# Order of the first batch: token-weight conversions placed behind the split of z, theta of block 1 ahead of attention of block 2

## The chip, the cores and the metric

One core of a Trainium2 chip runs one program. The metric is the device time of one execution in microseconds (us). TensorE (PE) multiplies matrices, VectorE (DVE) and ScalarE (ACT) do elementwise work, SyncE (SP) issues the transfers between memory and the on-chip buffers. Each engine works through its own list of instructions in the order in which they stand.

## The reference

All inputs are float32; batch B = 4, sequence S = 768, width 512 (8 heads of 64).

```python
# 1. attention by chunks of 32 queries; each sees 8 memory keys and a window of keys (16 left, 8 right)
a = softmax(q_c @ k_full.T / 8);  x = a @ v_full             # -> x[B, S, 512]
# 2. token mixing with a phase
theta = x @ w_theta
zr, zi = x * cos(theta), x * sin(theta)
y = w_tok_r @ zr + w_tok_i @ zi                              # over the 768 tokens
u = x + y;  x = u + relu(u @ w_ch)
# 3. gated block
h = gelu(x @ w_in);  u, v = halves of h
v = layernorm(v) * g_ln;  v = w_sg @ v + b_sg                # over the 768 tokens
out = x + (u * v) @ w_out
```

## The kernel before

**Precision.** A float32 operand of a matmul is split into a high part (rounded to the type float32r, by ScalarE) and a low part (operand minus high part, by VectorE). Each product is made of three: high by high, high by low, low by high.

**Tiles.** The 768 tokens of a batch are six blocks of 128. Blocks are counted from 0, over all batches. Per block the program runs, in functions of the same name:
- `att_s` (scores on PE into the PSUM tile `att2`, then maximum L245 and subtraction L247 on DVE, Exp L251 on ACT),
- `att_t` (transposes L258 of p on PE, copy L262 to `pt` on ACT),
- `att_v` (p times v on PE, again into `att2`; reciprocal of the row sum and L274 on DVE give x in `xt`),
- `att_x` (transposes L284 on PE, split into `xhi` by ACT L112 and `xlo` by DVE L113),
- `theta` (twelve matmuls L311; reduction to a turn, L322 and L325, on DVE into `t`; two Sin, L327 and L335, on ACT; z = x times them, L336, on DVE),
- `z_split` (high part L348 on ACT, two low parts L350 on DVE),
- `mix_group` (six matmuls L378 for each of four accumulators: 24 a block).

`att2`, `p`, `pt`, `t` and the PSUM tile of `theta` have one buffer each. The accumulators of mixing take all four buffers of `acc`, over all six blocks.

**Token weights.** `w_tok` comes as twelve pieces of 128x768 float64 values (six blocks for each half of the output tokens). `tok_conv` takes the next piece: it makes float32 high and low parts from the bits of the raw words, and asks for the load of the piece two further on (`raw` has three buffers, `cvh` two). Up to the second piece (`convert_pe`) the low part is made on PE, later (`convert`) on DVE: L150 and L203 on ACT, L153, L156, L160, L204, L208 and L209 on DVE. Mixing of block 0 with the first half needs the first piece, of block 1 the second, and so on.

**What sets the order.** `net_kernel` writes the work down step by step (the lines below), and a list scheduler takes that sequence as priorities. At each engine it takes the instruction of the highest priority whose operands it reckons to be there. So a line moved in the program changes the order of instructions on every engine, on SP's list of transfers too, also in places that the diff does not show. The first batch has a lead-in written out call by call, and then a loop over units `it` of mixing, with four groups `q` in each; `run` holds the pieces of attention, which are bound to a step and a group.

Of the kernel before, what the change touches and what calls it, by code (L numbers as in the profile page):

```python
# [32 lines left out]
def net_kernel(tc, qt, kw, vw, ident, w_theta, w_tok, w_ch, w_in, w_sg, w_out, g_ln, b_sg, out):  # L33
# [7 lines left out]
    AO, CO = -4, -2  # L41
# [8 lines left out]
    def r32(ap):  # L50
        return ap.bitcast(F32)
# [25 lines left out]
    def slot(n, tag, dtype=F32R):  # L77
        return w1.tile([128, n], dtype, tag=tag, name=tag, bufs=NBLK + 2)

    def two(t, i, n):  # L80
        return t[:, 2 * n * i:2 * n * i + 2 * n].rearrange("p (r t) -> p r t", r=2)
# [26 lines left out]
    def th_tile():  # L108
        return ps.tile([128, 512], F32, tag="th", name="th", bufs=1)

    def split(hi, lo, src, eng=None):
        nc.scalar.activation(out=hi, in_=src, func=AF.Copy)  # L112
        (eng or nc.vector).tensor_tensor(out=lo, in0=src, in1=r32(hi), op=ALU.subtract)  # L113
# [103 lines left out]
    def load_att(i):  # L217
        q = at.tile([128, NPAIR, 128], F32, tag="q", name="q", bufs=NQ)
        nc.sync.dma_start(out=q, in_=qt[i].rearrange("p (a t) -> p a t", a=NPAIR))
        q_t[i] = q  # L220
        nc.sync.dma_start(out=ka[i % NK], in_=kw[i])

    def load_v(i):
        nc.sync.dma_start(out=va[i % NKV], in_=vw[i])
# [71 lines left out]
    NFIRST = 2 * NBLK  # L296

    def has_theta(n):
        return 0 <= n < NBLK or NFIRST <= n < len(units)

    def theta(n):
        b, d0, nd, s, _ = units[n]
        xt, (_, xhi, xlo) = xt_of[b % 2][s], sets[b % 2]
        nz = 128 * nd
        cols = slice(128 * d0, 128 * d0 + nz)
        tok = slice(128 * s, 128 * s + 128)
        th = th_tile()[:, 0:nz]
        i = 0
        for k in range(KD):
            for a, w in ((xhi, th_hi), (xhi, th_lo), (xlo, th_hi)):  # L310
                nc.tensor.matmul(  # L311
                    out=th, lhsT=a[:, k, tok], rhs=w[:, k, cols],
                    start=(i == 0), stop=(i == 3 * KD - 1),
                )
                i += 1
        if n < NFIRST + 2:
            t = wk.tile([128, 512], F32, tag="t", name="t", bufs=1)[:, 0:nz]
        else:
            if len(t_slots) < 2:
                t_slots.append(slot(512, "slot_x", F32))  # L320
            t = t_slots[n % 2][:, 256 * (n // 2 % 2):256 * (n // 2 % 2) + 256]
        nc.vector.tensor_scalar(  # L322
            out=t, in0=th, scalar1=MAGIC, scalar2=MAGIC, op0=ALU.add, op1=ALU.subtract
        )
        nc.vector.tensor_tensor(out=t, in0=th, in1=t, op=ALU.subtract)  # L325
        z = wk.tile([128, 2, 512], F32, tag="z", name="z", bufs=ZB)[:, :, 0:nz]
        nc.scalar.activation(out=z[:, 1], in_=t, func=AF.Sin, scale=TWO_PI)  # L327
        if n < NBLK:
            nc.scalar.activation(out=z[:, 0], in_=t, func=AF.Abs)
        else:  # L330
            nc.vector.tensor_scalar(
                out=z[:, 0].bitcast(I32), in0=t.bitcast(I32), scalar1=0x7FFFFFFF, scalar2=None,
                op0=ALU.bitwise_and,
            )
        nc.scalar.activation(out=z[:, 0], in_=z[:, 0], func=AF.Sin, scale=-TWO_PI, bias=halfpi)  # L335
        nc.vector.tensor_tensor(  # L336
            out=z, in0=z, in1=xt[:, cols].unsqueeze(1).to_broadcast([128, 2, nz]), op=ALU.mult
        )
        sc_t[n] = z

    def z_split(n):
        z = sc_t.pop(n)
        if n < NBLK:
            a, b = slot(3 * 512, "slot"), slot(512, "slot_x")
            hi = two(a, 0, 512)
            lo = a[:, 1024:], b
            z_t[n] = z_t[n + NBLK] = (hi[:, 0], hi[:, 1]), lo
            nc.scalar.activation(out=hi, in_=z, func=AF.Copy)  # L348
            for i in range(2):
                (nc.gpsimd if n < -9 else nc.vector).tensor_tensor(  # L350
                    out=lo[i], in0=z[:, i], in1=r32(hi[:, i]), op=ALU.subtract
                )
            return
        if len(z_slots) < 2:
            z_slots.append(slot(3 * 512, "slot"))
        i = n % 3
        if i < 2:
            hi, lo = two(z_slots[i], 0, 256), two(z_slots[i], 1, 256)
        else:
            hi, lo = two(z_slots[0], 2, 256), two(z_slots[1], 2, 256)  # L360
        split(hi, lo, z)
        z_t[n] = (hi[:, 0], hi[:, 1]), (lo[:, 0], lo[:, 1])

    def mix_group(n, g):
        b, d0, nd, s, halves = units[n]
        d2, th = divmod(g, len(halves))
        th = halves[th]
        first, last = s == 0, s == NBLK - 1
        if first:
            acc_t[g] = acc_tile()  # L370
        zhi, zlo = z_t[n]
        whi, wlo = tok_w[s][th]
        acc = acc_t[g]
        zc = slice(128 * d2, 128 * d2 + 128)
        i = 0
        for ri in range(2):
            for z, w in ((zhi, whi), (zhi, wlo), (zlo, whi)):
                nc.tensor.matmul(  # L378
                    out=acc[:, 0:TC], lhsT=z[ri][:, zc], rhs=w[:, ri],
                    start=(first and i == 0), stop=(last and i == 5),  # L380
                )
                i += 1
        if last:
            _, xhi, xlo = sets[b % 2]
            dt = d0 + d2
            tt = slice(TC * th, TC * th + TC)
            u = wk.tile([128, TC], F32, tag="u", name="u", bufs=2)
            nc.vector.tensor_tensor(out=u, in0=acc[:, 0:TC], in1=r32(xhi[:, dt, tt]), op=ALU.add)
            (nc.gpsimd if b >= 4 else nc.vector).tensor_tensor(out=u, in0=u, in1=r32(xlo[:, dt, tt]), op=ALU.add)  # L389
            nc.sync.dma_start(out=u_dram[2 * b + th][:, dt, :], in_=u)  # L390
        if g == 3:
            z_t.pop(n)
# [237 lines left out]
    def run(it, slot):  # L630
        for fn, i in pieces.get((it, slot), []):
            if i < NA:
                fn(i)

    if True:
# [8 lines left out]
        def place(s):  # L644
            t = slot(3 * 512, "slot")
            tok_w[s][1] = two(t, 0, TC), two(t, 1, TC)
            xt_of[1][s] = slot(512, "slot_x", F32)
            w1s.pieces[NTH + NBLK + s] = tok_piece(s, 1)
# [31 lines left out]
        def tok_conv():  # L680
            nonlocal jw
            if jw >= NTH + NBLK:
                place(jw - NTH - NBLK)
            if jw < NTH + 2:
                w1s.convert_pe(jw, bank=acc_tile)
            else:
                w1s.convert(jw)
            w1s.load(jw + 2)
            jw += 1

        def att(part, i):
            part(i)
            if part is att_s:
                load_att(i + NK)
            if part is att_v:
                load_v(i + NKV)
# [10 lines left out]
        th_conv()  # L707
        theta(0)
        att(att_t, 1)
        tok_conv()  # L710
        att(att_v, 1)
        att(att_x, 1)
        z_split(0)
        att(att_s, 2)
        theta(1)
        tok_conv()
        att(att_t, 2)
        att(att_v, 2)
        z_split(1)
        att(att_s, 3)  # L720
        for it in range(NU):
            run(it, -2)
            run(it, -1)
            for q in range(4):
                if has_theta(it + 2) and q == (3 if it < NBLK else 0):
                    theta(it + 2)
                run(it, q)
                if it >= 0:
                    mix_group(it, q)
                if it < CO + NFIRST and q == 3:  # L730
                    tok_conv()
                if last_att + 2 <= it < last_att + 6 and q % 2:
                    j = 2 * (it - last_att - 2) + q // 2
                    p2["w"].convert(j)
                    p2["w"].load(j + NRAW)
                if has_theta(it + 2) and q == 3:
                    z_split(it + 2)
            run(it, 9)
            if it == NFIRST + CO - 1:
                close(st_cm)  # L740
                s1_cm, set1 = opened("set1")
                sets[1] = x_set(set1, 1, None)
            if it == last_att + 1:
                close(at_cm)
                close(s0_cm)
                open_p2()
                load_u(0)
                load_u(1)
                load_u(2)
            if it == last_att + 6:  # L750
                split_u(0)
# [142 lines left out]
```

## Time and profile before

| what | value |
|---|---|
| time, median of three runs (lowest to highest) | 758.88 us (755.14 to 758.88) |
| the profiled execution: its own time, its span | 762.43 us, 760.6 us |
| mean granted TensorE clock in the span | 0.993 of full speed |
| busy: PE / DVE / ACT | 730.4 us (96%) / 488.0 us (64%) / 306.9 us (40%) |
| chain that ended last: PE / DVE / DMA / ACT | 70% / 17% / 6% / 4% |

Busy shares are means over the whole span. The first 100 us or so, in which attention, theta, z and the conversion of token weights of the first batch all run, differ from the rest: there VectorE is nearly full as well. Times in the rows count from the start of the span. The end of a matmul is modelled, and instructions of one engine overlap a little, so that steps from start to start are what one of them costs.

### The profile page before, as it was taken

What the parts mean: (1) busy time and instruction counts of PE and PEld (TensorE: products, weight loads), DVE (VectorE), ACT (ScalarE), POOL (GpSimd) and SP (SyncE); (2) the same over time, 40 slices, a digit from 0 to 9 for tenths busy, and PEclk for the clock granted to TensorE, in tenths of its full rate; (3) what the DMA queues carried; (4) which work ended last, traced back from release to release, by engine and by line L of the source; (5) the groups of instructions that cost most, each with busy time, mean ns of one, the idle gap of its engine ahead of it and who ended that gap; (6) DMA issues with size and microseconds to landing.
All of it is one profiled execution on the core that took longest, in us unless ns stands there. A gap on an engine that the chain in (4) does not pass through costs nothing.

```text
span 760.6 us, 16131 instructions
## 1 busy us (share of the span) xinstructions
PE 730.4 (96%) x6968; PEld 680.7 (89%) x6968; DVE 488.0 (64%) x920; ACT 306.9 (40%) x470; POOL 0.3 (0%) x6
## 2 busy tenths in 40 slices
PE   5989999999999999999998899999999999999998
PEld 2667888889999999999998798999899989998997
DVE  4999898757566575798469777754355435543452
ACT  4867544554554554453125325611251134113310
POOL 0000000000000000000000000000000000000000
PEclk9998999999999999999999999999999999999999
DMA  8685465423323330341069755003100310030002
GB/s 345 226 288 163 151 224 182 142 72 129 123 85 127 112 113 30 102 177 43 11 226 328 276 185 158 1 0 115 53 1 1 114 53 1 1 125 0 1 1 84
DMA packets 33047, 86.90 MB, mean 114 GB/s; under 512 B 3792, under 2 KB 16208, under 8 KB 32976
## 3 DMA queue, kind: packets, MB, share of 16 engines
q1 hardware_dynamic: 30384, 77.22, 29.3%
q10 hardware_dynamic: 2592, 8.65, 3.6%
q8 instruction: 55, 0.90, 0.5%
q14 instruction: 16, 0.13, 0.1%
HBM read 66.98 MB, written 18.87 MB: 113 GB/s over the span
## 4 chain that ended last, share of the span: by engine, by line
PE 70%; DVE 17%; DMA 6%; ACT 4%; issue 2%; SPq 0%; DVEq 0%; ACTq 0%
PE acc L378 15%; PE acc L569 13%; PE acc L506 9%; PE acc L544 9%; PE acc L589 9%; PE th L311 7%; PE acc L432 3%; PE att L234 3%; DMA raw<-w_in 2%; DVE cvh L156 2%; DVE cvh L208 1%; DVE z L336 1%; PE att L258 1%; DVE cvm L204 1%; DVE u L389 1%
## 5 line engine op out<-in xcount | busy, mean ns | idle before, releaser
L378 PE MATMUL acc<-tok,slot 128*128 128x384 f32 x552 | 116.7, 342 | 2.5 <-ACT slot L348 2.5
L378 PE MATMUL acc<-slot 128*128 128x384 f32 x552 | 115.6, 340 | 0.0
L378 PEld LDWEIGHTS acc<-tok,slot 128*128 128x128 f32 x552 | 94.6, 188 | 4.6 <-ACT slot L348 2.8
L378 PEld LDWEIGHTS acc<-slot 128*128 128x128 f32 x552 | 95.5, 188 | 1.7
L569 PE MATMUL acc<-sg_hi,vlo 128*128 128x384 f32 x192 | 64.5, 336 | 0.0
L569 PE MATMUL acc<-sg_hi,vhi 128*128 128x384 f32 x192 | 64.4, 336 | 0.0
L569 PE MATMUL acc<-sg_lo,vhi 128*128 128x384 f32 x192 | 64.4, 336 | 0.0
L311 PE MATMUL th<-th_hi,xhi 128*128 128x256 f32 (+1 forms) x168 | 52.8, 314 | 1.6 <-ACT xhi L112 1.3
L112 ACT ACTIVATE ghi<-g 128x384 fp32r<-128x384 f32 x32 | 16.8, 525 | 88.0 <-DVE g L578 88.0
L311 PE MATMUL th<-th_hi,xlo 128*128 128x256 f32 (+1 forms) x168 | 51.4, 306 | 0.4 <-DVE xlo L113 0.4
L574 DVE SCALAR_TENSOR_TENSOR g<-acc,g_col,b_bc 128x384 f32<-128x384 f32 x32 | 19.8, 617 | 48.7 <-PE acc L569 48.7
L311 PE MATMUL th<-th_lo,xhi 128*128 128x256 f32 (+1 forms) x168 | 50.7, 302 | 0.0
L432 PE MATMUL acc<-ulo,ch_hi 128*128 128x384 f32 x128 | 43.7, 342 | 4.1 <-DVE ulo L113 4.1
L432 PE MATMUL acc<-uhi,ch_hi 128*128 128x384 f32 x128 | 43.7, 342 | 2.3 <-DVE x2e L438 2.3
L432 PE MATMUL acc<-uhi,ch_lo 128*128 128x384 f32 x128 | 43.4, 339 | 0.0
L544 PE MATMUL acc<-x3lo,in_hi 128*128 128x384 f32 x128 | 43.1, 336 | 0.0
L544 PE MATMUL acc<-x3hi,in_hi 128*128 128x384 f32 x128 | 43.1, 336 | 0.0
L544 PE MATMUL acc<-x3hi,in_lo 128*128 128x384 f32 x128 | 43.1, 336 | 0.0
L589 PE MATMUL acc<-glo,out_hi 128*128 128x384 f32 x128 | 43.0, 336 | 0.0
L589 PE MATMUL acc<-ghi,out_lo 128*128 128x384 f32 x128 | 43.0, 336 | 0.0
L589 PE MATMUL acc<-ghi,out_hi 128*128 128x384 f32 x128 | 42.9, 336 | 0.0
L595 DVE TENSOR_TENSOR o<-acc,x3f 128x384 f32<-128x384 f32 x32 | 17.8, 555 | 37.3 <-PE acc L589 37.3
(141 smaller groups left out, 1564.1 us busy)
## 6 DMA issues: line engine op xcount, KB each, us to landing
va<-vw SPq DMA_DIRECT2D x24, 520.0 KB, 4.0
ka<-kw SPq DMA_DIRECT2D x24, 512.0 KB, 4.8
raw<-w_tok SPq DMA_DIRECT2D x12, 768.0 KB, 5.1
q<-qt SPq DMA_DIRECT2D x24, 256.0 KB, 2.9
u_dram<-u SPq DMA_DIRECT2D x32, 192.0 KB, 2.1
uf<-u_dram SPq DMA_DIRECT2D x8, 768.0 KB, 7.9
x_dram<-x2e SPq DMA_DIRECT2D x32, 192.0 KB, 4.1
x3f<-x_dram SPq DMA_DIRECT2D x8, 768.0 KB, 4.7
```

Of the source, the lines that this page charges most:

```text
L112: nc.scalar.activation(out=hi, in_=src, func=AF.Copy)
L156: nc.vector.scalar_tensor_tensor(out=h, in0=high, scalar=-0x80000000, in1=h, op0=ALU.bitwise_and, op1=ALU.bitwise_or,)
L234: nc.tensor.matmul(out=out[32 * c:32 * c + 32, j, n * a:n * a + n], lhsT=lhs[h, a, 32 * c:32 * c + 32], rhs=rhs[h, 4 * a + c, :], start=Tr ...
L311: nc.tensor.matmul(out=th, lhsT=a[:, k, tok], rhs=w[:, k, cols], start=(i == 0), stop=(i == 3 * KD - 1),)
L378: nc.tensor.matmul(out=acc[:, 0:TC], lhsT=z[ri][:, zc], rhs=w[:, ri], start=(first and i == 0), stop=(last and i == 5),)
L432: nc.tensor.matmul(out=acc[:, 0:TC], lhsT=w[:, k, ee], rhs=x[:, k, :], start=(i == 0), stop=(i == 3 * KD - 1),)
L506: nc.tensor.matmul(out=acc, lhsT=x[:, k, tt], rhs=w[:, k, :], start=(i == 0), stop=(i == 3 * KD - 1),)
L544: nc.tensor.matmul(out=acc[:, 0:TC], lhsT=w[:, k, ff], rhs=x[:, k, :], start=(i == 0), stop=(i == 3 * KD - 1),)
L569: nc.tensor.matmul(out=acc[:, 0:TC], lhsT=v, rhs=w, start=(i == 0), stop=(i == 3 * NBLK - 1))
L574: nc.vector.scalar_tensor_tensor(out=g, in0=acc[:, 0:TC], scalar=p3["g"][:, f:f + 1], in1=p3["b"][:, tt], op0=ALU.mult, op1=ALU.add,)
L589: nc.tensor.matmul(out=acc[:, 0:TC], lhsT=w[:, k, ee], rhs=x[:, k, :], start=(i == 0), stop=(i == 3 * KD - 1),)
L595: nc.vector.tensor_tensor(out=o, in0=acc[:, 0:TC], in1=p3["xr"][c][:, e, :], op=ALU.add)
```

## The change

In the lead-in the first `tok_conv` goes behind `z_split(0)` and the second behind `att_t` of block 2; `theta(1)` goes ahead of `att_s` of block 2 and `z_split(1)` behind it. In the loop `tok_conv` of a step goes behind `z_split` of that step. No operation is added or removed.

```diff
         th_conv()
         theta(0)
         att(att_t, 1)
-        tok_conv()
         att(att_v, 1)
         att(att_x, 1)
         z_split(0)
+        tok_conv()
+        theta(1)
         att(att_s, 2)
-        theta(1)
+        z_split(1)
+        att(att_t, 2)
         tok_conv()
-        att(att_t, 2)
         att(att_v, 2)
-        z_split(1)
         att(att_s, 3)
...
-                if it < CO + NFIRST and q == 3:
-                    tok_conv()
...
                 if has_theta(it + 2) and q == 3:
                     z_split(it + 2)
+                if it < CO + NFIRST and q == 3:
+                    tok_conv()
```

What the scheduler makes of it is shown at three places. The number behind a tile's name tells buffers apart: `z_493` before and `z_452` after are z of block 1, `p_471` and `p_492` the scores of block 2, `cvh_747` and `cvh_752` the third piece of token weights, `cvh_902` and `cvh_907` the fourth, `att2_525` and `att2_530` the values of block 2.

ScalarE, from the high part of z of block 0 to the last Sin of block 1, before:

```order
L348 ACTIVATE slot_431<-z_354 128x1024
L150 ACTIVATE cvh_747<-raw_384 128x768
L251 ACT_TABLE_LOAD
L251 ACTIVATE p_471<-p_471 128x512
L190 ACTIVATE tok1_1_105<-acc_506 128x384
L190 ACTIVATE tok1_1_105<-acc_511 128x384
L327 ACT_TABLE_LOAD
L327 ACTIVATE z_493<-t_490 128x512
L329 ACTIVATE z_493<-t_490 128x512
L262 ACTIVATE pt_523<-att_518 128x512
L335 ACTIVATE z_493<-z_493,halfpi_98 128x512
```

The same stretch after:

```order
L348 ACTIVATE slot_411<-z_354 128x1024
L150 ACTIVATE cvh_752<-raw_434 128x768
L190 ACTIVATE tok1_1_105<-acc_518 128x384
L190 ACTIVATE tok1_1_105<-acc_523 128x384
L150 ACTIVATE cvh_907<-raw_528 128x768
L327 ACTIVATE z_452<-t_449 128x512
L329 ACTIVATE z_452<-t_449 128x512
L251 ACT_TABLE_LOAD
L251 ACTIVATE p_492<-p_492 128x512
L335 ACT_TABLE_LOAD
L335 ACTIVATE z_452<-z_452,halfpi_98 128x512
L262 ACTIVATE pt_508<-att_503 128x512
```

The Exp of block 2 with its table load stood ahead of both Sin of block 1; now it stands between them, with a table load on either side. The first step of the fourth piece (L150 on `raw_528`) has come ahead of the Sin, and the copy L262 of block 2 has gone behind the last Sin.

VectorE, from the subtraction of block 2's maximum to x of block 2, before:

```order
L247 TENSOR_TENSOR p_471<-att2_436,mx_469 128x2x4x64
L153 TENSOR_SCALAR cvh_747<-cvh_747 128x768
L322 TENSOR_SCALAR t_490<-th_477 128x512
L156 SCALAR_TENSOR_TENSOR cvh_747<-raw_384,cvh_747 128x768
L325 TENSOR_TENSOR t_490<-th_477,t_490 128x512
L160 TENSOR_SCALAR cvm_748<-cvh_747 128x768
L204 SCALAR_TENSOR_TENSOR cvm_748<-raw_384,cvm_748 128x768
L336 TENSOR_TENSOR z_493<-z_493,xt1_115 128x1024
L270 TENSOR_SCALAR rs_558<-att2_525 128x8
L208 TENSOR_TENSOR cvh_747<-cvh_747,tok0_2_106 128x768
L273 RECIPROCAL rs_558<-rs_558 128x8
L209 TENSOR_TENSOR tok1_2_107<-cvh_747,cvm_748 128x768
```

From the same instruction after:

```order
L247 TENSOR_TENSOR p_492<-att2_457,mx_490 128x2x4x64
L153 TENSOR_SCALAR cvh_752<-cvh_752 128x768
L153 TENSOR_SCALAR cvh_907<-cvh_907 128x768
L156 SCALAR_TENSOR_TENSOR cvh_752<-raw_434,cvh_752 128x768
L156 SCALAR_TENSOR_TENSOR cvh_907<-raw_528,cvh_907 128x768
L160 TENSOR_SCALAR cvm_753<-cvh_752 128x768
L160 TENSOR_SCALAR cvm_908<-cvh_907 128x768
L204 SCALAR_TENSOR_TENSOR cvm_753<-raw_434,cvm_753 128x768
L204 SCALAR_TENSOR_TENSOR cvm_908<-raw_528,cvm_908 128x768
L336 TENSOR_TENSOR z_452<-z_452,xt1_115 128x1024
L208 TENSOR_TENSOR cvh_752<-cvh_752,tok0_2_106 128x768
L270 TENSOR_SCALAR rs_563<-att2_530 128x8
```

Eight instructions of the third and fourth piece now stand between block 2's scores and z of block 1, where four of the third piece stood. L322 and L325 of block 1 have gone ahead of L247 (they stand just above these rows). Behind these rows L208 and L209 of the fourth piece follow around L274 of block 2, where before the fourth piece was only begun.

SyncE, the transfers from the second load of v for an odd block on, as a difference:

```order
 L221 DMA ka_123<-kw 128x1024
-L139 DMA raw<-w_tok 128x1536
 L224 DMA va_125<-vw 128x1040
+L139 DMA raw<-w_tok 128x1536 x2
 L219 DMA q<-qt 128x512
 L221 DMA ka_122<-kw 128x1024
```

The load of the third piece has gone behind a load of v, which waits until `att_v` of block 1 has read its buffer; the load of the fourth piece follows it at once, ahead of the keys and queries of block 4.

## Rows read from the trace of the kernel before

**Rows 1.** Windows: stretch, length, busy us of PE, PEld, DVE, ACT, POOL; clock; DMA.

```profile
100.00:120.00 20.00, 18.85 (x405) 16.95 (x405) 20.00 (x34) 7.84 (x11) 0.00 (x0) 1.00 0.70 229
...
220.00:300.00 80.00, 79.13 (x1153) 74.57 (x1152) 50.62 (x105) 41.84 (x63) 0.00 (x0) 1.00 0.32 103
```

**Rows 2.** Timeline of PE: start us, length us, instruction xcount, [idle before <- releaser].

```profile
36.71 1.04 PE L378 MATMUL acc<-tok,slot 128*128 128x384 f32 x5
...
43.54 1.69 PE L378 MATMUL acc<-tok,slot 128*128 128x384 f32 x8 [1.25 <-ACT slot L348]
...
57.73 0.63 PE L284 MATMUL att<-id_sb,xt 128*128 128x128 f32 x4 [2.25 <-DVE xt L274]
...
60.12 0.80 PE L311 MATMUL th<-th_hi,xhi 128*128 128x512 f32 x1 [0.65 <-ACT xhi L112]
...
66.20 0.86 PE L234 MATMUL att<-va,pt 64*32 64x65 f32 x64
67.00 1.14 PE L378 MATMUL acc<-tok,slot 128*128 128x384 f32 x5
...
91.18 2.00 PE L378 MATMUL acc<-tok,slot 128*128 128x384 f32 x10 [1.22 <-ACT slot L348]
```

**Rows 3.** Windows, PE alone: stretch, length, busy us, granted clock, DMA share, GB/s.

```profile
56.00:58.00 2.00, 0.27 (x3) 1.00 0.68 254
58.00:60.00 2.00, 1.47 (x68) 0.57 0.42 54
...
62.00:64.00 2.00, 2.00 (x8) 0.50 0.96 296
64.00:66.00 2.00, 2.00 (x8) 0.73 0.37 149
```

**Rows 4.** Timeline of PE, theta matmuls at either clock.

```profile
63.53 0.63 PE L311 MATMUL th<-th_lo,xhi 128*128 128x512 f32 x1
63.95 0.63 PE L311 MATMUL th<-th_hi,xlo 128*128 128x512 f32 x1
...
75.41 0.40 PE L311 MATMUL th<-th_hi,xlo 128*128 128x512 f32 x1
75.64 0.39 PE L311 MATMUL th<-th_hi,xhi 128*128 128x512 f32 x1
```

**Rows 5.** Timeline of ACT around the Sin of block 1.

```profile
37.44 1.28 ACT L327 ACT_TABLE_LOAD   x1
38.74 0.63 ACT L327 ACTIVATE z<-t 128x512 f32<-128x512 f32 x1
...
40.27 0.71 ACT L335 ACTIVATE z<-z,halfpi 128x512 f32<-128x512 f32 x1
...
42.44 1.05 ACT L348 ACTIVATE slot<-z 128x1024 fp32r<-128x1024 f32 x1
```

**Rows 6.** Timeline of DVE from z of block 1 to x of block 3.

```profile
41.02 1.23 DVE L336 TENSOR_TENSOR z<-z,xt 128x1024 f32<-128x1024 f32 x1 [1.11 <-ACT z L335]
...
43.39 0.96 DVE L209 TENSOR_TENSOR tok<-cvh,cvm 128x768 fp32r<-128x768 f32 x1
44.27 0.68 DVE L274 TENSOR_TENSOR xt<-att,rs 128x512 f32<-128x512 f32 x1
...
48.00 0.68 DVE L247 TENSOR_TENSOR p<-att,mx 128x512 f32<-128x512 f32 x1
...
49.67 0.55 DVE L153 TENSOR_SCALAR cvh<-cvh 128x768 int32<-128x768 int32 x1
50.14 0.95 DVE L204 SCALAR_TENSOR_TENSOR cvm<-raw,cvm 128x768 f32<-128x768 uint32 x1
...
56.90 0.68 DVE L274 TENSOR_TENSOR xt<-att,rs 128x512 f32<-128x512 f32 x1
```

**Rows 7.** The page's DMA issues, loads of token weights: xcount, KB each, us to landing.

```profile
raw<-w_tok SPq DMA_DIRECT2D x12, 768.0 KB, 5.1
```

**Rows 8.** Timeline of SP's queue: the load of v behind att_v of block 1.

```profile
28.83 0.33 SPq L224 DMA_DIRECT2D va<-vw  x1
```

## The prediction

> **What bounds the kernel now.** I read the windows first, to see which engine is full in which stretch. From 100 to 120 us VectorE is busy for all of 20 us and PE for 18.85; from 220 to 300 us PE is busy for 79.13 of 80 us and VectorE for 50.62 [rows 1]. So the two engines bound the first batch together, and behind it PE alone does. The change reorders the first batch only, and whatever makes PE late there arrives at the end undiminished, unless PE gets it back before some 125 us.
>
> Then I read PE's timeline for its gaps, since these are what a new order can win or add. Between 36 and 92 us the large ones are 1.25 us ahead of mixing block 1 (it waits for the high part of z), 2.25 us ahead of the transposes of block 3 (for x on VectorE), 0.65 us ahead of theta of block 3, and 1.22 us ahead of mixing block 5 [rows 2]. They add up to 5.37 us.
>
> Then I read the clock. In the stretch that holds the 2.25 us gap PE is busy for 0.27 of 2 us, still at a granted 1.00, which is 2.4 GHz. Behind it the clock goes to 0.50, 1.2 GHz: means of 0.57, 0.50 and 0.73 in windows of 2 us [rows 3]. Theta of block 3 runs in that time: from start to start its matmuls take 0.42 us there and 0.23 us at the full clock [rows 4]. Ten of them at 0.19 us more are 1.9 us that the gap costs beyond itself.
>
> **The change part by part.** All operations stay, so nothing is saved on any engine; only waits can change. I follow the new lists by hand from 36 us, with durations from start to start: L153 0.47 us, L204 0.87 (0.95 less the overlap of 0.08), L209 0.88, operations on 512 columns such as L274 0.60 (0.68 less 0.08) [rows 6]. L160 is taken like L153, L156 like L204 and L208 like L209, whose shapes they have.
>
> *Z of block 1.* VectorE now takes L322 and L325 of block 1 ahead of the scores of block 2, but theta itself waits for the same x as before, and mixing block 0, which started at 36.71 us [rows 2], stood four short matmuls behind it; so theta ends at about 36.2 us. Four operations of 0.60 us follow, the last of them L247 of block 2, until 38.6 us. On ScalarE the L190 ahead of the table load ended at 37.4 us [rows 5]; now L150 of the fourth piece comes there, some 0.9 us, and the first Sin follows at 38.3 us. That holds if this piece has landed. The load of v that it stands behind went out at 28.83 us [rows 8], two loads of 768 KB follow, the second by about 31 us, and the median to landing is 5.1 us [rows 7]: 36.1 us, 1.3 us to spare, so I cost it at nothing; each microsecond beyond that would hold the Sin by one.
>
> Before, the first Sin began at 38.74 us and the last at 40.27 us [rows 5]. Now L327 and L329 end at 39.4 us, then come a table load, Exp (0.6 us) and a second table load; from a load's start to the start of the Sin behind it are 1.30 us [rows 5]. The last Sin starts at 39.4 + 1.30 + 0.6 + 1.30 = 42.6 and ends at 43.3 us. VectorE meanwhile does four instructions of each of two pieces: 2 x (0.47 + 0.87 + 0.47 + 0.87) = 5.4 us, from 38.6 to 44.0 us. So L336 starts at 44.0 us and not at 41.02 [rows 6]: 3.0 us late.
>
> The Trainium skill (ScalarE: Activation LUTs, What ACT_TABLE_LOAD costs) puts a switch of the table set at 1.28 us for the load and about 1.38 us for a drain, 2.66 us together. The trace has the load at 1.28 us but the next Sin 0.02 us behind it [rows 5], so it shows no such drain. By the page, as an estimate, the last Sin would end 2.7 us later than above and L336 start 2.0 us later; the sum goes by the row.
>
> *PE, blocks 1 and 2.* Mixing block 0 starts at about 36.9 us; 24 matmuls at 0.175 us (five in a row last 1.04 us [rows 2], the first 0.34 of it) are 4.2 us, until 41.1 us. Before, the transposes of block 2 lay inside that. Now they wait for Exp until 41.4 us, the copy to `pt` waits on ScalarE behind the last Sin until 43.9 us, att_v (0.86 us [rows 2]) runs from 44.0 us, and mixing block 1 waits for its high part: L336 ends at 45.15 us, and L348 (1.05 us [rows 5]) behind L203 of the fourth piece at 46.4 us. So PE stands for 0.3 + 2.1 + 1.6 = 4.0 us where it stood for 1.25 [rows 2], and mixing block 1 starts 2.9 us later than at 43.54.
>
> *Block 3.* Behind L336 VectorE does L208 and L209 of the third piece, two L350, L208 of the fourth, the two short ones of block 2's row sum, and then L274 of block 2: 45.15 + 3 x 0.88 + 1.2 + 0.2 = 49.2 us, 4.9 us later than at 44.27 [rows 6]. The scores of block 3 can only start when that has emptied `att2`, at 49.8 us. VectorE has L209, L153, L156 and two of 0.60 us until L247 of block 3: 49.8 + 3.4 = 53.2 us, where it was 48.00 [rows 6]. Then, until x of block 3, come four operations of 0.60, L208 and L209, two L160, L153, L204, L156 and a row sum, 7.5 us: x of block 3 starts at 61.3 us instead of 56.90 [rows 6]. PE has no mixing left to fill in: all of block 1 and theta of block 2 are done by about 58 us, so it waits until 62.0 us, about 4 us instead of 2.25 [rows 2].
>
> *What comes back.* At 62 us VectorE has the fifth piece done and the sixth begun, about 4 us of work that it did later before. So what follows is faster. Theta of block 3 waits for its high part until 64.4 us. If the clock falls again as it did behind the gap of before, ten matmuls take 4.2 us, att_v of block 4 ends at 71.4 us, and mixing block 2 starts then, 4.4 us later than at 67.00 [rows 2]; at the full clock 69.4 us. From there to mixing block 5 PE needed 24.2 us before, of which 1.22 us were the last wait [rows 2] and, by my count of the matmuls, half a microsecond smaller ones. The last wait goes: the high part of z of block 5 is 6 us behind the end of its theta, and PE has 30 matmuls and one att_s ahead of it, 6.1 us. So block 5 starts at 71.4 + 22.5 = 93.9 us, or at 69.4 + 22.5 + 1 (x of block 4 is then late) = 92.9 us, against 91.18 [rows 2]: 1.7 to 2.7 us late, and I take 2.3, nearer to the case with the clock down, as a gap like it brought the clock down before.
>
> Behind that both lists have the same work for VectorE, which is full there [rows 1]; of PE's 1.15 us idle in that window I let 0.2 us come back. **The sum is 2.3 - 0.2 = 2.1 us longer.** Against the profiled execution that is 762.43 + 2.1 = 764.5 us; this execution was 3.55 us above the median of the runs shown, and against the median it is 758.88 + 2.1 = 761.0 us. The other places that change order (attention of the second batch between 90 and 200 us) move instructions of PE past each other by a few matmuls; PE is full there and I cost them at nothing, with 0.5 us to either side.
>
> The bounds: 0, if VectorE's lead pays it all back; 4.5 us, with the clock down once more, below.
>
> **The rivals.**
>
> *The clock falls twice: slower.* From 41.1 to 46.4 us PE would be busy for 1.3 of 5.3 us. If the clock falls behind that too, 17 mixing matmuls of block 1 run at twice 0.175 us: 3.0 us more, of which the wait for `att2` hides 0.3. The scores of block 3 come 2.7 us later, x of block 3 about 2.4 us later, since VectorE has a little other work to put in, and the second fall remains: 2.1 + 2.4 = 4.5 us, 763.4 us. It decides if the granted clock goes to 0.50 at some point from 44 to 52 us. Against it: att_v runs in the middle, and behind the gap of 1.25 us the clock did not fall before.
>
> The Trainium skill (TensorE: Matmul & The Clock Gate, Terms) prices throttled time at that time multiplied by one minus the granted ratio. The fall of before, some 6.8 us by its three windows [rows 3], would be 3.4 us by that, as an estimate, and this rival 2.1 + 3.4 = 5.5 us; the rows show 1.9 us, as PE waited or fed VectorE in the rest of it.
>
> *VectorE's lead removes the gap: faster.* With two pieces further converted, x of block 3 could come ahead of PE's need; then the wait of 2.25 us, the 1.9 us of low clock behind it and the 0.65 us of theta go: 4.8 us, of which about 0.5 us is spent at block 1. 758.9 - 4.3 = 754.6 us. For it: conversions are the bulk of VectorE's work here. Against it: the list has x of block 3 behind the fifth piece and parts of the sixth, and it hangs on scores that start 4.9 us late.
>
> *Nothing moves.* PE and VectorE have the same work until 125 us and are both nearly full; what PE loses at block 1 it gets back by block 5, as the pieces are ready. 758.9 us.
>
> **How the numbers follow.** The forecast has 0.50, the clock falling twice 0.27, the lead that removes the gap 0.11, nothing moved 0.12. About 0.5% (3.8 us) is what a measurement of this kernel can tell from no change. Above 762.7 us lies the clock rival but for 0.02, and 0.07 of the forecast's upper end: 0.32. Below 755.1 us lies nearly all of the faster rival: 0.10. Between them is 0.58. The forecast's own range is 759.5 to 763 us. The range for 8 in 10 takes in the clock rival with half a microsecond for other places and a late landing of the fourth piece, and reaches to the lead on the other side: 755.5 to 766 us.
>
> **What would show it.** Right: on ScalarE the last Sin of block 1 ending behind 43 us, with a table load on either side of Exp; on PE a wait of about 2 us ahead of att_v of block 2 and one of about 4 us ahead of the transposes of block 3; mixing block 2 starting near 71 us and block 5 near 93.5 us; windows from 220 us on as before. Wrong: the first Sin waiting for the load of the fourth piece; mixing block 2 starting ahead of 67 us; the clock at 1.00 throughout; or a gap behind 130 us that before does not have.

## The result and the profile after

The changed kernel takes 764.18 us in the median of six runs (762.16 to 766.64); the kernel before, run beside it, 757.59 us (755.14 to 759.53). The ratio is 1.0084, 95% interval [1.0058, 1.011]: slower by 6.4 us, between 4.4 and 8.3. The time lies inside the forecast's range (755.5 to 766.0), but above the point forecast of 761.0 us and beyond the likeliest case's own range; of the cases it is nearest to the rival in which the clock falls twice (763.4 us).

The two profiled executions can't be compared by their clock times as they stand. Up to the turn of block 0 (L325) VectorE has the same list in both, and yet it makes this turn at 27.19 us in the profile of before and at 24.88 us in that of after. So I count from this instruction. Two marks behind it are the first sum u of the first batch (L388), which VectorE makes when the first accumulator is complete, and the first sum of the second batch. The second mark is the safer one: at the first one PE has not done the same work in every kernel, at the second it has done the same 416 matmuls of mixing (L378) in all of them. Timeline of VectorE, L325 and the two marks, before:

```profile
27.19 0.69 DVE L325 TENSOR_TENSOR t<-th,t 128x512 f32<-128x512 f32 x1
...
93.40 0.55 DVE L388 TENSOR_TENSOR u<-acc,xhi 128x384 f32<-128x384 f32 x1
...
182.13 0.56 DVE L388 TENSOR_TENSOR u<-acc,xhi 128x384 f32<-128x384 f32 x1 [0.27 <-PE acc L378]
```

The same view after, with z of block 1, x of block 2, the scores and x of block 3 between:

```profile
24.88 0.68 DVE L325 TENSOR_TENSOR t<-th,t 128x512 f32<-128x512 f32 x1
...
41.50 1.22 DVE L336 TENSOR_TENSOR z<-z,xt 128x1024 f32<-128x1024 f32 x1
...
46.63 0.68 DVE L274 TENSOR_TENSOR xt<-att,rs 128x512 f32<-128x512 f32 x1
...
51.20 0.69 DVE L245 TENSOR_REDUCE mx<-att 128x8 f32<-128x512 f32 x1 [1.55 <-PE att L234]
...
61.08 0.68 DVE L274 TENSOR_TENSOR xt<-att,rs 128x512 f32<-128x512 f32 x1
...
97.14 0.56 DVE L388 TENSOR_TENSOR u<-acc,xhi 128x384 f32<-128x384 f32 x1 [0.16 <-PE acc L378]
...
185.22 0.56 DVE L388 TENSOR_TENSOR u<-acc,xhi 128x384 f32<-128x384 f32 x1 [0.27 <-PE acc L378]
```

From L325 to the first sum it is 66.21 us before and 72.26 us after, 6.05 us more; to the second batch's first sum 154.94 and 160.34 us, 5.4 us more. So the loss arises in the first batch, 0.65 us of it comes back, and the rest lies inside the interval of the times. Nothing is added later: from 220 to 300 us PE is busy for 79.15 us, as in [rows 1].

```profile
220.00:300.00 80.00, 79.15 (x1153) 74.64 (x1153) 51.53 (x106) 41.17 (x62) 0.00 (x0) 1.00 0.32 104
```

Timeline of ScalarE around the Sin of block 1, after; it answers to [rows 5]:

```profile
36.07 0.64 ACT L327 ACTIVATE z<-t 128x512 f32<-128x512 f32 x1
...
37.25 1.28 ACT L251 ACT_TABLE_LOAD   x1
38.54 0.63 ACT L251 ACTIVATE p<-p 128x512 f32<-128x512 f32 x1
39.19 1.28 ACT L335 ACT_TABLE_LOAD   x1
40.49 0.72 ACT L335 ACTIVATE z<-z,halfpi 128x512 f32<-128x512 f32 x1
41.11 0.58 ACT L262 ACTIVATE pt<-att 128x512 f32<-128x512 f32 x1
...
43.06 1.04 ACT L348 ACTIVATE slot<-z 128x1024 fp32r<-128x1024 f32 x1
```

Exp with a table load on either side stands between the two Sin (L327 and L335), and the copy to `pt` (L262) and the high part of z (L348) come behind them. PE's timeline after shows who waits for those two; it answers to [rows 2]:

```profile
41.74 0.86 PE L234 MATMUL att<-va,pt 64*32 64x65 f32 x64 [1.86 <-ACT pt L262]
44.15 3.25 PE L378 MATMUL acc<-tok,slot 128*128 128x384 f32 x9 [1.55 <-ACT slot L348]
...
47.52 1.16 PE L378 MATMUL acc<-tok,slot 128*128 128x384 f32 x3
48.48 0.52 PE L378 MATMUL acc<-tok,slot_x 128*128 128x384 f32 x1
...
50.30 0.86 PE L234 MATMUL att<-ka,q 64*32 64x64 f32 x64
...
61.91 1.08 PE L284 MATMUL att<-id_sb,xt 128*128 128x128 f32 x4 [3.39 <-DVE xt L274]
...
71.70 1.15 PE L378 MATMUL acc<-tok,slot 128*128 128x384 f32 x5
...
94.75 2.18 PE L378 MATMUL acc<-tok,slot 128*128 128x384 f32 x11 [0.57 <-ACT slot L348]
```

These are two waits of 1.86 and 1.55 us with one att_v between them, then mixing block 1 at a slow step (three matmuls from 47.52 to 48.48 us, 0.32 us each, where [rows 2] give 0.175), and the scores of block 3 (50.30 us) behind it. VectorE waits 1.55 us for those scores (L245 above). The windows of PE after (stretch, length, busy us, granted clock, DMA share, GB/s) say why the step is slow:

```profile
42.00:44.00 2.00, 0.61 (x61) 0.78 0.85 332
44.00:46.00 2.00, 1.85 (x6) 0.50 0.85 300
...
48.00:50.00 2.00, 2.00 (x8) 0.51 0.22 87
...
60.00:62.00 2.00, 0.09 (x1) 0.55 0.97 360
...
70.00:72.00 2.00, 2.00 (x70) 0.89 0.00 0
```

The clock falls twice: from 42 to 50 us, and from 60 to 71 us (0.50 in all the windows left out), longer than in [rows 3]. Before, it stayed at 1.00 from 42 to 58 us; the window behind the 1.25 us wait ahead of mixing block 1:

```profile
44.00:46.00 2.00, 2.00 (x72) 1.00 0.55 199
```

### The profile page after: what moved, and what is told of

Same layout as the page of the kernel before. It is cut to its first block, busy times and chain, and to the rows that moved or that the text cites. A ratio compares the mean times of both kernels' runs of the same rounds, so it can differ in the third digit from the quotient of the medians.

```text
span 762.5 us, 16132 instructions
## 1 busy us (share of the span) xinstructions
PE 731.6 (96%) x6968; PEld 683.1 (90%) x6968; DVE 488.4 (64%) x920; ACT 306.8 (40%) x470; POOL 0.3 (0%) x6
## 4 chain that ended last, share of the span: by engine, by line
PE 75%; DVE 12%; ACT 6%; DMA 4%; issue 2%; SPq 0%; ACTq 0%; DVEq 0%
PE acc L378 19%; PE acc L569 13%; PE acc L506 9%; PE acc L544 9%; PE acc L589 9%; PE th L311 8%; PE acc L432 3%; PE att L234 3%; DMA raw<-w_in 2%; DVE cvh L156 1%; PE att L284 1%; PE att L258 1%; DVE z L336 1%; ACT L327 1%; DVE cvm L204 1%
## 5 line engine op out<-in xcount | busy, mean ns | idle before, releaser
L378 PE MATMUL acc<-tok,slot 128*128 128x384 f32 x552 | 118.4, 346 | 2.1 <-ACT slot L348 2.1
L378 PE MATMUL acc<-slot 128*128 128x384 f32 x552 | 116.6, 340 | 0.0
L378 PEld LDWEIGHTS acc<-tok,slot 128*128 128x128 f32 x552 | 96.9, 192 | 3.7 <-ACT slot L348 2.4
L378 PEld LDWEIGHTS acc<-slot 128*128 128x128 f32 x552 | 96.0, 188 | 1.6
```

Source lines behind the costliest of these rows:

```text
L378: nc.tensor.matmul(out=acc[:, 0:TC], lhsT=z[ri][:, zc], rhs=w[:, ri], start=(first and i == 0), stop=(last and i == 5),)
```

## The experiments

The theories were these. **W**: the loss is the chain of waits that begins with Exp and its two table loads between the Sin of block 1, that is, with theta put ahead of the scores. **V**: the loss is the new place of the conversions and their loads. **C**: the gaps lower PE's clock, and that costs on top of the waits.

The edit of the loop needs no theory: a kernel with it alone has, row by row, the lists of before on every engine. All that moves comes from the lead-in. Its time is the last experiment. One line of the lead-in is in none of the partial kernels e1, e2, e8 and e9: `z_split(1)` ahead of `att_t` of block 2. For each kernel two measures are given: the ratio of the times, and the stretch from L325 to the first sum; a table behind the last experiment adds the second mark.

### e1_theta: theta of block 1 ahead of the scores, alone

```diff
-        att(att_s, 2)
         theta(1)
+        att(att_s, 2)
```

> Before with one part of the change: theta of block 1 ahead of att_s of block 2, both conversions of the lead-in where they were. In its list Exp of block 2 lies between the two Sin of block 1, as in the changed kernel, and VectorE has most of two pieces ahead of L336 of block 1. Theory W (the wait chain: Exp with its two table loads inside theta of block 1, so that z, mixing block 1 and x of block 2 come late): near the changed kernel, 762 to 765 us, with a PE gap of 2 us or more ahead of mixing block 1. Rival V (the place of the conversions and of their loads costs the time): near the kernel before, 756 to 759 us.

Ratio 1.0064 [1.0041, 1.0087]; to the first sum (24.88 to 94.65 us) 69.77 us, 3.6 more than before. PE's timeline and one window:

```profile
42.18 1.05 PE L234 MATMUL att<-va,pt 64*32 64x65 f32 x64 [1.86 <-ACT pt L262]
44.65 3.57 PE L378 MATMUL acc<-tok,slot 128*128 128x384 f32 x10 [1.42 <-ACT slot L348]
...
60.56 1.09 PE L284 MATMUL att<-id_sb,xt 128*128 128x128 f32 x4 [2.78 <-DVE xt L274]
```

```profile
44.00:46.00 2.00, 1.35 (x4) 0.50 0.79 243
```

The waits ahead of blocks 1 and 2 and the first fall of the clock are there in full without the conversions having moved. W holds for the beginning of the loss; the wait for block 3 is 0.6 us shorter than in the changed kernel.

### e2_conv: the conversions, alone

```diff
         att(att_t, 1)
-        tok_conv()
         att(att_v, 1)
         att(att_x, 1)
         z_split(0)
+        tok_conv()
         att(att_s, 2)
         theta(1)
-        tok_conv()
         att(att_t, 2)
+        tok_conv()
         att(att_v, 2)
```

> Before with the other part of the change: both conversions of the lead-in moved as in the change, theta of block 1 left behind att_s of block 2. Exp stands ahead of both Sin as before, att_v of block 2 comes in the middle of mixing block 0. Theory W: no loss, 755 to 759 us. Rival V: the loss stays, 762 to 765 us.

Ratio 0.9972 [0.9953, 0.9991]; to the first sum 64.62 us, 1.6 less than before. ScalarE has Exp ahead of both Sin again:

```profile
34.46 0.63 ACT L251 ACTIVATE p<-p 128x512 f32<-128x512 f32 x1
35.11 1.28 ACT L327 ACT_TABLE_LOAD   x1
```

V falls: the moved conversions by themselves cost nothing and may give a little. The changed kernel needs 2.5 us more to the first sum than e1. It has the conversions and `z_split(1)` in their new places besides theta, and no run tells what each of the two has in these 2.5 us.

### e3_abs: the changed kernel without Exp between the Sin

Between the two Sin of a block stands an Abs (L329) that needs only the turn. It is written ahead of the first Sin, and the scheduler then keeps the Sin together. The edit holds for all six blocks of the first batch; in its rows Abs is L328 and the first Sin L329.

```diff
-        nc.scalar.activation(out=z[:, 1], in_=t, func=AF.Sin, scale=TWO_PI)
         if n < NBLK:
             nc.scalar.activation(out=z[:, 0], in_=t, func=AF.Abs)
-        else:
+        nc.scalar.activation(out=z[:, 1], in_=t, func=AF.Sin, scale=TWO_PI)
+        if n >= NBLK:
...
```

> The changed kernel with Abs ahead of the first Sin in theta: the two Sin then stand back to back, the list puts Exp behind the last Sin, and half a piece instead of two ahead of L336. Nothing is left out. Theory W: z of block 1 comes about 3 us earlier than in the changed kernel, mixing block 1 follows block 0 almost without a gap, 757 to 760 us. Rival V: little changes, 762 to 765 us, as the loads and the lead-in's conversions are where the change put them.

Ratio 0.9998 [0.9978, 1.0018]: by the times the loss is gone. Timelines of ScalarE and of VectorE's marks:

```profile
38.26 0.61 ACT L329 ACTIVATE z<-t 128x512 f32<-128x512 f32 x1
38.78 0.71 ACT L335 ACTIVATE z<-z,halfpi 128x512 f32<-128x512 f32 x1
39.50 1.28 ACT L251 ACT_TABLE_LOAD   x1
...
41.34 1.04 ACT L348 ACTIVATE slot<-z 128x1024 fp32r<-128x1024 f32 x1
```

```profile
27.04 0.68 DVE L325 TENSOR_TENSOR t<-th,t 128x512 f32<-128x512 f32 x1
...
93.06 0.56 DVE L388 TENSOR_TENSOR u<-acc,xhi 128x384 f32<-128x384 f32 x1 [0.24 <-PE acc L378]
...
183.61 0.56 DVE L388 TENSOR_TENSOR u<-acc,xhi 128x384 f32<-128x384 f32 x1 [0.27 <-PE acc L378]
```

One table load instead of two, and Exp behind both Sin; the high part of z (L348) starts 14.30 us behind L325, where after has 18.18 us. PE's waits for Exp and for mixing block 1 are 0.38 and 0.29 us, and the clock stays at 1.00 from 42 to 56 us. The wait for x of block 3 remains (3.33 us), and with it one fall of the clock. To the first sum it is 66.02 us against 66.21 before, but this mark flatters e3: PE has done 126 matmuls of mixing by then, and 133 before. To the second batch's first sum it is 156.57 us, against 154.94 before and 160.34 after: by the trace 3.8 of the 5.4 us come back. W is shown for the changed kernel: with the beginning mended, most of the loss goes by the trace, and all of it within the interval of the times.

### e4_fill: dummy work in the gaps

The changed kernel, with transposes whose result nothing reads (`filler`, L228) at block 2, 15 ahead of att_v and 12 ahead of the transposes of x, and at block 3, 4 ahead of att_v and 28 behind it.

```diff
+    def filler(out, src, n):
+        for _ in range(n):
+            nc.tensor.transpose(out=out, in_=src, identity=id_sb)
...
+        filler(pv_t[:, 0, 0:128], last["p"][:, 0:128], {2: 15}.get(i, 0))
...
+        filler(tp[:, 0:128], last["pt"][:, 0, :], {2: 12, 3: 32}.get(i, 0))
```

> The changed kernel with transposes that nothing reads in PE's gaps: 15 of p behind the transposes of block 2, 12 of pt behind att_v of block 2, 32 of pt ahead of the transposes of block 3. They add work for PE where it waits and leave the waits of other engines alone. Theory C (each gap lowers the clock, and that costs on top of the wait): the granted clock stays at 1.00 through 40 to 72 us and 3 to 4 us come back, 760 to 761 us. Theory W without C (VectorE paces the stretch and the low clock lies under its waits): 763 to 766 us, clock or no clock.

Ratio 1.0021 [1.0004, 1.0037]: work was added, and 0.63% of the time came back. PE's timeline and windows:

```profile
40.39 1.80 PE L228 MATMUL att<-id_sb,p 128*128 128x128 f32 x15
42.42 0.86 PE L234 MATMUL att<-va,pt 64*32 64x65 f32 x64 [0.23 <-ACT pt L262]
```

```profile
44.00:46.00 2.00, 1.62 (x11) 1.00 0.99 406
46.00:48.00 2.00, 2.00 (x12) 1.00 1.00 400
...
64.00:66.00 2.00, 1.58 (x6) 0.56 0.99 362
66.00:68.00 2.00, 2.00 (x6) 0.58 0.47 181
```

Att_v still waits for ScalarE, but the clock stays up until 64 us, and only a short fall is left. VectorE and ScalarE work through the same lists as in the changed kernel, so that what comes back is not another order there. On PE the scores of block 3 have moved ahead of three matmuls of mixing, which is 0.5 us at 0.175 us each; not all that comes back must be the clock. C is shown: part of the loss is the clock and not the waits. How large that part is, the two measures put differently: 4.8 us by the times (0.0063 of 759 us), 2.7 us to the first sum (72.26 to 69.53 us), and as much to the second mark.

### e5_fill12 and e6_fill3: the two falls apart

The fillers of e4 at block 2 alone, and at block 3 alone.

> The changed kernel with fillers (transposes whose result nothing reads) at block 2 alone, 15 ahead of att_v and 12 ahead of the transposes of x; none at block 3. Run e4, which had fillers at both, was 1.0021 of the kernel before where the changed kernel is 1.0084. C1, most of what the clock costs lies in the first fall (42 to 50 us): the clock stays at 1.00 from 40 to 52 us, the fall behind block 3 (58 to 71 us) stays as long as it was; ratio 1.002 to 1.004. C2, the second, longer fall costs most: ratio 1.006 to 1.008. W, waits alone count: 1.008 or above, since fillers add work.

> The changed kernel with 32 fillers at block 3 alone, 4 ahead of att_v and 28 behind it. C1, the first fall costs most: the clock falls at 42 to 50 us as in the changed kernel, and the one behind block 3 is shorter than 13 us; ratio 1.005 to 1.008. C2: the second fall costs most, ratio 1.001 to 1.003. The two theories give runs e5 and e6 in opposite order. If the two falls add up, (ratio e5 - 1.0021) + (ratio e6 - 1.0021) is about 1.0084 - 1.0021 = 0.006.

Ratios 1.0062 [1.0035, 1.009] and 1.0062 [1.0041, 1.0084]: the times don't tell the two falls apart, and C1's range for e5 (1.002 to 1.004) is missed. To the first sum it is 69.72 us with the first fall removed (2.5 us less than after) and 71.61 us with fillers at block 3 alone (0.65 us less); to the second mark 1.4 and 0.5 us less. So the first fall is the dearer one by the traces, as C1 says, but the runs do not part the two cleanly: in e5 the second fall is shorter as well (0.94, 0.50, 0.50, 0.50 and 0.85 in the windows from 60 to 70 us), and in e6 it is only shortened. By the times this stays open, and neither run alone has a gain beyond the intervals.

What the first fall does to block 3 is seen in e5 (scores of block 3 on PE, x of block 3 on VectorE; L325 is at 25.99 us):

```profile
48.83 0.86 PE L234 MATMUL att<-ka,q 64*32 64x64 f32 x64
...
59.95 0.68 DVE L274 TENSOR_TENSOR xt<-att,rs 128x512 f32<-128x512 f32 x1
```

With the clock up the scores start 22.84 us behind L325, where after has 25.42, VectorE has no wait for them, and x of block 3 comes at 33.96 us instead of 36.20. As in e4, 0.5 us of this may be the three matmuls that the scores have passed.

### e7_abs_before: Abs first without the change

> The kernel before with the Abs of a block given ahead of its first Sin, and nothing of the change. Run e3 took the changed kernel from 1.0084 to 0.9998 by this line. W, the line helps only where an Exp falls between the two Sin of a block; before, the Exp of block 2 stands ahead of both, so nothing is to be won: ratio 0.997 to 1.002. Rival, back to back Sin are a gain of their own (the first Sin no longer has Abs behind it): ratio 0.992 to 0.996, and then run e3 was that gain set against an unmended loss.

Ratio 1.0043 [1.0016, 1.007]; to the first sum 67.25 us, 1.0 more than before, and as much to the second mark. Both theories missed by the ratio. W (up to 1.002) missed by little, as 1.0 us is 0.14% of the time and the last experiment widens all intervals by 0.2%. ScalarE's timeline, and PE's:

```profile
36.85 0.64 ACT L328 ACTIVATE z<-t 128x512 f32<-128x512 f32 x1 [1.06 <-DVE t L325]
37.51 1.28 ACT L329 ACT_TABLE_LOAD   x1
...
39.34 0.71 ACT L335 ACTIVATE z<-z,halfpi 128x512 f32<-128x512 f32 x1
```

```profile
40.58 0.86 PE L234 MATMUL att<-va,pt 64*32 64x65 f32 x64 [0.72 <-ACT pt L262]
43.06 2.01 PE L378 MATMUL acc<-tok,slot 128*128 128x384 f32 x10 [1.61 <-ACT slot L348]
```

Abs waits 1.06 us for the turn, and the table load stands behind it. In [rows 5] the load is the first in the row, from 37.44 us, and ran while VectorE made the turn (L325 of block 1, from 37.76 us). The last Sin starts 13.76 us behind L325 of block 0 (25.58 us here), before 13.08 us. So the line is no cure as such: it helped where it kept an Exp out from between the Sin, and cost where the table had to be changed anyway. PE's two waits, with the same att_v between them as in the changed kernel, left the clock at 1.00 here (all windows from 40 to 56 us).

### e8_conv_abs and e9_theta_abs: Abs first with one half of the change

> A candidate for a version better than both: the kernel before with the two conversions of the lead-in moved (run e2, 0.9972) and Abs ahead of the first Sin; theta of block 1 stays behind the scores of block 2. W: in run e2 the Exp already stands ahead of both Sin, so the line adds nothing: 0.995 to 0.999. Rival, the two gains add up: below 0.995. If the longer way of an Exp past two Sin lets a new gap arise on PE: above 1.000, and the clock shows a second fall.

> Theta of block 1 ahead of the scores of block 2 (run e1, 1.0064), with Abs ahead of the first Sin; the conversions of token weights stand as before. W, the loss of e1 is the Exp with two table loads between the two Sin: the Sin stand back to back, the first gap (1.86 + 1.42 us ahead of att_v of block 2 and of mixing block 1) shrinks below 1.5 us in sum, the clock stays at 1.00 from 40 to 52 us; ratio 0.997 to 1.002. Rival from run e7 (1.0043): Abs first puts a table load behind the wait for the turn, and this is paid here too: 1.003 to 1.006.

With the conversions: 1.0021 [0.9997, 1.0045], to the first sum 66.60 us; the line takes away what e2 had. The table load stands behind Abs here too, and the last Sin of block 1 starts 12.95 us behind L325, in e2 12.41; but this Abs has no wait for the turn, so that the reason of e7 is not shown for it. A second fall of the clock, which the last of the expectations had, it is not (there is one, from 56 to 60 us). With theta: 1.004 [1.0023, 1.0056], to the first sum 68.48 us. There the Sin are back to back and the clock stays at 1.00 from 40 to 60 us, as W said; but gaps of 0.90 us (Exp of block 2), 1.10 us (scores of block 4) and 3.22 us (x of block 3) remain. Of e1's 3.6 us to the first sum 1.3 come back, with 129 matmuls of mixing done by then where e1 has 134; at the second mark nothing does (158.18 us, e1 157.87). W's number for the time missed, and the rival's range held, though its reason is not seen at block 1, where Abs has no wait for the turn. So Exp between the Sin explains the two waits and the first fall of e1, but not its lateness at the end of the batch. Why the line helps the full change and not theta alone was not taken apart further; the conversions and `z_split(1)` are what differs.

### e10_loop: the loop's edit alone

> The kernel before with the edit of the loop alone (each conversion behind the split of z); the lead-in stays. Its lists on PE, VectorE, ScalarE and SyncE are those of before. All theories: 1.000, with an interval that holds 1; a ratio outside 0.998 to 1.002 would say that the intervals of all runs are to be widened by as much.

Ratio 1.0021 [1.0003, 1.0039]: not 1, with lists that are those of before. VectorE's marks:

```profile
25.11 0.69 DVE L325 TENSOR_TENSOR t<-th,t 128x512 f32<-128x512 f32 x1
...
91.47 0.55 DVE L388 TENSOR_TENSOR u<-acc,xhi 128x384 f32<-128x384 f32 x1
```

It is 66.36 us against 66.21, and 155.31 against 154.94 at the second mark: the trace repeats to 0.2 and 0.4 us although the beginning differs by 2.1 us. It does not repeat to the end: from L325 to the end of the span it is 733.4 us before and 729.2 us here, with the same lists. So marks are compared here and not spans. The 0.2% of the times have no place in the profile that I found; buffers have other numbers in this kernel, which was not followed up. For the rest it means that ratios within some 0.2% of each other or of 1 prove nothing, that of e2 hardly more; what stands are after, e1, e3 and the step from after to e4. The best kernel run is e2, with the conversions moved and theta where it was; that it beats the kernel before rests on its time and on the 1.6 us to the first sum (1.7 to the second mark).

All kernels in the order of the second mark, us from L325:

| kernel | first sum | second batch's first sum | ratio of the times |
|---|---|---|---|
| e2_conv | 64.62 | 153.28 | 0.9972 |
| before | 66.21 | 154.94 | 1 |
| e10_loop | 66.36 | 155.31 | 1.0021 |
| e8_conv_abs | 66.60 | 155.42 | 1.0021 |
| e7_abs_before | 67.25 | 155.97 | 1.0043 |
| e3_abs | 66.02 | 156.57 | 0.9998 |
| e4_fill | 69.53 | 157.66 | 1.0021 |
| e1_theta | 69.77 | 157.87 | 1.0064 |
| e9_theta_abs | 68.48 | 158.18 | 1.0040 |
| e5_fill12 | 69.72 | 158.96 | 1.0062 |
| e6_fill3 | 71.61 | 159.81 | 1.0062 |
| after | 72.26 | 160.34 | 1.0084 |

## Why the prediction was right and wrong

To compare, 2.31 us are taken off the prediction's times (27.19 - 24.88).

**Z of block 1: right.** First Sin 36.0 us predicted, 36.07 measured; last Sin 40.3 and 40.49; L336 41.7 and 41.50. The fourth piece had landed in time, as costed: its L150 starts at 35.28 us without a wait.

The Trainium skill (ScalarE: Activation LUTs, What ACT_TABLE_LOAD costs) has a drain of about 1.38 us in each switch. With two switches in a row the trace still shows none: Exp ends at 39.17 us, the load starts at 39.19 and the Sin at 40.49 us. The row was the one to go by.

**PE, blocks 1 and 2: right.** The waits were predicted as 0.3 + 2.1 + 1.6 us; those of after are 1.86 and 1.55 us, with 0.20 us ahead of the transposes of block 2. Mixing block 1 was to start at 44.1 us and starts at 44.15.

**Block 3: its first half right, then wrong.** X of block 2 was predicted at 46.9 us and comes at 46.63. The scores of block 3 were to start at 47.5 us, and start at 50.30. This is the step that failed: it let PE do mixing block 1 at the full clock, and the clock was at 0.50 from 44 to 50 us. The likeliest case had left this first fall out, because behind the gap of 1.25 us before the clock had not fallen; two gaps with one att_v between them are another thing, and the prediction had itself counted PE as busy for 1.3 of 5.3 us there. VectorE then waited for PE (1.55 us), which no term of the sum had, as VectorE was reckoned the fuller engine there. X of block 3 came at 61.08 us, 2.1 us later than forecast (59.0); the rival of the falling clock had 2.4 us. Run e5, without the first fall, comes out near the forecast: counted from L325 the scores start at 22.84 us (forecast 22.6) and x of block 3 comes at 33.96 us (forecast 34.1).

**The order of the rivals.** So the mechanism was that of the rival to which 0.27 was given, with its own mark (the clock at 0.50 at some point from 44 to 52 us) met. The time lies in the stated range because the range took in this rival; the likeliest case, at 2.1 us, had a third of the loss. The rival's sum of 4.5 us was nearer, and still too small: 6.05 us at the first sum, 5.4 us in the second batch. Two terms are mis-sized. Mixing block 2 starts at 71.70 us, 2.6 later than forecast (69.1). From there to block 5 it is 23.05 us, where 22.5 were forecast: the wait ahead of block 5 was to go and is still 0.57 us, so block 5 is 5.9 us later than before, where the forecast had 2.3, taken between 2.7 with the clock down and 1.7 with it up. What comes back behind it is 0.65 us against the 0.2 forecast, with marks that repeat to 0.4 us.

The Trainium skill (TensorE: Matmul & The Clock Gate, Terms) prices throttled time at that time multiplied by one minus the granted ratio. By the windows after, the two falls are 3.4 and 5.1 us by that, as an estimate, 8.5 us together against 3.4 before: 5.1 us more. The fall that e4 keeps is 1.7 us, so that e4 would give back 6.8 us by the page, as an estimate. It gave back 4.8 us by the times and 2.7 us by the trace: the page's price is above what the runs show. Its price for the rival, 5.5 us, still came nearer to the measured 5.4 to 6.05 us than the sum by rows. As far as the runs show that is chance, since the terms named above were missing from that sum as well.

**The faster rival** was wrong in its premise: VectorE's lead in conversions did not bring x of block 3 forward; the wait for it grew from 2.25 [rows 2] to 3.39 us.

**The reading by clock times would have misled.** Mixing block 2 was forecast near 71 us and block 5 near 93.5 us, and the profile after shows 71.70 and 94.75: which looks like a match, because its execution was 2.31 us ahead at L325. The spans (760.6 and 762.5 us) differ by 1.9 us, near the forecast's 2.1, partly for the same reason: from L325 to the end it is 4.2 us more after, and the median times differ by 6.6 us.

## What to carry to other kernels

Cost a gap on TensorE together with the clock behind it, and do not take a lone gap that left the clock up as proof for several in a row: here two waits of 1.9 and 1.6 us began a loss of 6 us. A rule for when the clock falls does not come out of these runs. In code that a list scheduler orders, look at which instruction can slip between two that share an activation table; moving work ahead by priority let an Exp in, and one line that closed the place undid the loss by the times (0.9998 for 1.0084) and 3.8 of 5.4 us of it by the trace. The same line added 1.0 us in the trace of before, where there was no Exp to keep out, and brought nothing at the second mark with theta alone. Compare two profiles from an event ahead of the change, and not from the start of the span, and up to a mark at which the engine has done the same work in both.

## What the runs showed of the hardware

- The clock fell in the second of two waits of 1.86 and 1.55 us with an att_v of 0.86 us between them (0.78 in the window from 42 to 44 us). It stayed at 1.00 behind the 1.25 us of [rows 2], and behind waits of 0.72 and 1.61 us with the same att_v between them (e7).
- Transposes with no reader kept the clock at 1.00 through the same waits of ScalarE (e4, 44 to 48 us), and the kernel with this extra work was faster than without it (1.0021 against 1.0084).
- A table load waits with the instruction ahead of it in ScalarE's list: in e7 it started at 37.51 us behind an Abs that had waited for VectorE, though ScalarE had been idle for 1.06 us. The load needs none of VectorE's results: in [rows 5] it started at 37.44 us, ahead of the turn.
